# Delta-rule attention and hash-routed experts on one core: expert places by indirect scatter, columns of 106 rows, V subtracted by VectorE, PSUM banks dealt by the planner

## The chip, the core and the metric

The kernel runs on one core of one Trainium2 chip. The metric is device time in microseconds (us) of one execution; the median of several runs is given, and one further execution was recorded by the hardware profiler. Engines are called PE (TensorE, with its weight loads PEld), DVE or VectorE, ACT (ScalarE), POOL (GpSimd) and SP (SyncE, which only issues DMAs here).

## The reference

Two blocks follow one another. All numbers are fp32 but the token ids, which are int64.

```python
# attention: q, k, v are (4, 8, 768, 48), beta (4, 8, 768)
k_n = k / (norm(k, axis=-1) + 1e-6)
for t in range(768):
    y[:, :, t] = q_t @ state                       # state is (48, 48) for each batch and head
    v_old = k_n_t @ state
    state += beta_t * outer(k_n_t, v_t - v_old)
x = y.transpose(0, 2, 1, 3).reshape(3072, 384)
# experts: w1 is (8, 384, 1024), w2 (8, 1024, 384)
expert = token_ids * 2654435761 % 8
for e in range(8):
    rows = expert == e
    out[rows] = relu(x[rows] @ w1[e]) @ w2[e]
```

## The kernel before

**Attention.** The 768 steps are cut into 24 chunks of 32 tokens (`C`), and four chunks make a group (`GC`), so there are six groups. For a group the kernel does the following.

- `load_turn` loads K and Q rows through SP (1024 pieces of 192 bytes each), and `turn` transposes them on PE into a PSUM bank `z`, from which ACT copies them to `KQ`.
- `gram` forms the products K K^T and K Q^T of a chunk on PE, in two `z` banks. ACT copies the first kind to `GK`, VectorE masks the second kind into `GQ`. There are two `z` banks, given out in turn by a counter (`next_z`) when the work is listed.
- `inverse` solves the triangular system of the four chunks and all heads at once on VectorE: a transpose `NT`, a few small operations, then for each row j a multiplication into `tmp` (line 429) and an addition into `U` (line 426). The columns of `U` are taken in parts (`cols`): three for the first two groups, two for the others. Each part is a chain in which every step needs the one before; chains of different parts may be interleaved.
- `turn_back` transposes the result into `TU` (line 446), from which `spread_t` makes `Tz`.

`chunk(c)` then carries the state through one chunk, and each chunk needs the state of the one before. `ask` multiplies K and Q with the state on PE (line 466, into the banks psX and psY). The residual R is V minus the K product: for chunks 1 to 19, PE first puts -V into psX through a negated identity `nident` (line 484), `ask` adds to it, and ACT copies it out with its sign turned (line 488); for the last four chunks (`LATE`) VectorE subtracts (line 492). `solve` multiplies with `Tz` (503), ACT copies W (512), `update` forms the new state on PE (518), which ACT copies out in four pieces (533), and `answer` (541) completes the rows of x, which SP stores to a DRAM scratch.

**Places.** `routing` works out on VectorE, for each token, which expert it goes to and which place it gets there: an expert has `CAP` = 512 places of its own in four columns of 128 rows, and what lies over goes to blocks of 128 at the end. In a first part it finds each token's place. In a second part, run among the last chunks, it turns this round, so that each place knows its token: VectorE builds masks `hi` and `lo` (line 682) and PE multiplies them in 8 groups of three (48 matmul records, line 689), VectorE adds the results into `val` and derives `gidx` (row of the output) and `gx` (row of the scratch, whose order differs).

**Order.** All of this is listed as tasks with an engine, a cost in ns, and names that they read and write. `order()` plays the engines forward with these costs, always taking the ready task with the longest rest of work, and the instructions are then emitted in that order. So each engine's order is fixed at build, and each engine executes it in order.

**Experts.** When the last x row is stored, a loop over overflow blocks follows, as many as the token ids ask for. Then come the experts one after another: POOL gathers rows by indirect DMA (`gather`, line 854), PE transposes them (`turn`, 863), `gemm1` multiplies with w1 (line 870, 512 columns of places stream through PE) with the ReLU on ACT and VectorE in turn (873, 875), `gemm2` multiplies with w2 (line 881, one column of 128 places as weights, 384 columns streaming), ACT and VectorE copy out in turn (884), and POOL scatters the rows to the output (885). SP loads weights up to four experts ahead.

Of the kernel before, what the change touches and what calls it, by code (L numbers as in the profile page):

```python
# [18 lines left out]
def kernel(  # L19
# [11 lines left out]
    nc = tc.nc  # L31
# [11 lines left out]
    CAP = 512  # L43
    KT = CAP // P
    NOV = (N - CAP) // P
# [4 lines left out]
    x_dram = nc.dram_tensor("x_scratch", (N, DIN), F32, kind="Internal").ap()  # L50
    x_rows = x_dram.rearrange("(c p) e -> c p e", p=P)
# [6 lines left out]
    gidx = keep.tile([P, NHI], I32)  # L58
    gx = keep.tile([P, NHI], I32)
# [35 lines left out]
    with ExitStack() as phase1:  # L95
# [15 lines left out]
        rt = st  # L111
# [20 lines left out]
        GKs = tiles(2, "GK", [P, C, GC, HU, 2])  # L132
# [9 lines left out]
        zs = [ps.tile([P, BANK], F32, name=f"z{i}") for i in range(2)]  # L142
# [17 lines left out]
        nident = st.tile([P, P], F32)  # L160
# [10 lines left out]
        def task(eng, ns, reads, writes, emit, words=0, kb=0, more=0, boost=0):  # L171
            deps = {writer[r] for r in reads if r in writer}
            for w in writes:
                deps |= readers.get(w, set())
                if w in writer:
# [4 lines left out]
                              more=more, boost=boost))  # L180
# [5 lines left out]
            return i  # L186

        def order():
# [25 lines left out]
            fetched, issued, begun = 0, 0, []  # L214
            BLOCK, FETCH = 256, 3550.0
            have = 900.0
            done = []
            while len(done) < n:
                best = None
                for e, r in ready.items():  # L220
                    if r:
                        at = max(free[e], min(x for x, _ in r))
                        if best is None or at < best[0]:
                            best = (at, e)
                at, e = best
                r = ready[e]
                pick = max((i for x, i in r if x <= at), key=lambda i: rest[i])

                soon = [(x, i) for x, i in r
                        if at < x < at + 0.7 * tasks[pick]["ns"] and rest[i] > rest[pick]]  # L230
                if soon:
                    x1 = min(x for x, _ in soon)
                    fits = [i for x, i in r if x <= at and tasks[i]["ns"] <= x1 - at + 60]
                    if fits:
                        pick = max(fits, key=lambda i: rest[i])
                    else:
                        free[e] = x1
                        continue
                t = tasks[pick]
                r.remove(next(p for p in r if p[1] == pick))  # L240
                s = at
                if e == "PE" and t["words"]:

                    blk = (issued + t["words"]) // BLOCK
                    while len(begun) <= blk:
                        m = len(begun)
                        t0 = have if m < 2 else max(have, begun[m - 1])
                        have = t0 + FETCH
# [5 lines left out]
                fin = s + t["ns"]  # L254
                if t["kb"]:
                    dma = max(dma, fin + 1500.0) + t["kb"] * 6.3
                    end[pick] = dma + 500.0 - LAG["SP"]
                else:
                    end[pick] = fin
# [29 lines left out]
        zn = [0]  # L289

        def next_z():
            zn[0] += 1
            return (zn[0] - 1) % 2

        def turn(g, a, b):
            z, KQ, src = next_z(), KQs[g % 4], (KTs, QTs)[a][b]
            pt = zs[z].rearrange("p (u x) -> p u x", u=HU)

            def go():
                for u in range(HU):  # L300
                    nc.tensor.transpose(pt[:, u, :], src[:, u].rearrange("p r d -> p (r d)"),  # L301
                                        ident)

            task("PE", 780, (f"t{a}{b}",), (f"z{z}",), go, words=8)
            task("ACT", 600, (f"z{z}",), (f"KQ{g % 4}{a}{b}",),
                 lambda: nc.scalar.activation(KQ[:, :, a, b, :], pt, ACT.Copy))  # L306
# [4 lines left out]
        def gram(c, parts=(0, 1)):  # L311

            g, cc = divmod(c, GC)
            KQ, tk, GK, GQ = KQs[g % 4], tokens(c), GKs[g % 2], GQs[c % 12]
            zz = [next_z(), next_z()]
            pg = [zs[z].rearrange("p (u a y) -> p u a y", u=HU, a=2, y=DP)[:, :, :, 0:C]
                  for z in zz]
            a0, a1 = parts[0], parts[-1] + 1
            held = tuple(f"KQ{g % 4}{a}{b}" for a in {0, *parts} for b in range(B))
            banks = tuple(f"z{z}" for z in zz)  # L320

            def go(u):
                for r in range(2):
                    for b in range(B):
                        nc.tensor.matmul(  # L325
                            pg[r][quarter(b), u, a0:a1], lhsT=KQ[half(r), u, 0, b, tk],
# [3 lines left out]
            for u in range(HU):  # L330
                task("PE", 300, held, banks, lambda u=u: go(u), words=32)
            for r in range(2):
                if 0 in parts:
                    task("ACT", 200, (banks[r],), (f"GK{g % 2}{cc}{r}",),
                         lambda r=r: nc.scalar.activation(
                             GK[:, :, cc, :, r].rearrange("p j u -> p u j"), pg[r][:, :, 0],
                             ACT.Copy))
            for r in range(2):
                if 1 in parts:
                    task("DVE", 200, (banks[r],), (f"GQ{c % 12}{r}",),  # L340
                         lambda r=r: nc.vector.tensor_tensor(  # L341
                             GQ[:, :, r], pg[r][:, :, 1],
                             mask[:, None, :].to_broadcast([P, HU, C]), op=ALU.mult),
                         boost=1e6)
# [17 lines left out]
        def spread_t(c):  # L362
            g, x0 = c // GC, H * (c % GC)
            spread((f"TU{g % 2}",), f"Tz{c % 2}", Tzs[c % 2], TUs[g % 2][:, x0:x0 + H],
# [11 lines left out]
        def inverse(g):  # L376
# [3 lines left out]
            cols = ((0, L // 2), (L // 2, L), (L, C)) if g < 2 else ((0, L), (L, C))  # L380
            parts = tuple(f"U{i}{c0 // (L // 2)}" for c0 in range(0, C, L // 2))

            def covered(c0, c1):
                return tuple(f"U{i}{c // (L // 2)}" for c in range(c0, c1, L // 2))

            def dve(ns, reads, writes, emit):
# [3 lines left out]
            task("DVE", 1240, tuple(f"GK{i}{cc}{r}" for cc in range(GC) for r in range(2)),  # L390
                 (f"NT{i}",), lambda: nc.vector.transpose(
                     NT, GKs[i].rearrange("p j c u r -> p j (c u r)")))
# [23 lines left out]
            for j0, j1, i0 in ((0, L, 1), (L, C - 1, L + 1)):  # L416
                task("DVE", 70 + 1.04 * (j1 - j0) * (C - i0), (f"NT{i}", f"nd{i}"),
                     (f"Ni{i}{j0}",), lambda j0=j0, j1=j1, i0=i0: nc.vector.tensor_tensor(
                         Ni[:, j0:j1, i0:], NT[:, j0:j1, i0:],
# [558 lines left out]
```

## Time and profile before

| | |
|---|---|
| median of 3 runs | 623.17 us (622.58 to 624.02) |
| profiled execution | 623.59 us, its span 622.0 us |
| granted TensorE clock, mean | 0.925 |
| PE busy | 565.7 us (91%) in 6810 instructions |
| VectorE busy | 263.8 us (42%) in 983 |
| ACT busy | 177.7 us (29%) in 390 |
| POOL busy | 87.3 us (14%) in 99 |
| DMA | 59.39 MB in 121561 packets |

The span runs from the first to the last instruction. A row of engines in 40 slices gives the busy share in tenths. A group's row names its line, engine, operation, what it writes and reads, its shape, how often it ran, then its busy time and the mean of one in ns, then the idle time before it. A row of the waits gives who waited for what: total us, times, the longest.

### The profile page before, as it was taken

To read this page: it belongs to the slowest core of one execution; us is meant where nothing else is said; L and a number is where in the kernel's file an instruction comes from. 1 tells how busy PE (TensorE), PEld (TensorE's weight loads), DVE (VectorE), ACT (ScalarE), POOL (GpSimd) and SP (SyncE) were. 2 spreads that over 40 slices of the span, in tenths; PEclk is the share of its full clock that TensorE was granted. 3 is DMA by queue.
4 is the path that set the end of the run, shared out by engine and by line. 5 is a ranking of instruction groups with operands and counts; after the bars stand their busy time and mean duration, and the time that the engine had idled before them with its cause. 6 is when DMAs were issued, how large, how long until landed. Compare 5 with 4: busy or idle time off the path is not lost.

```text
span 622.0 us, 16113 instructions
## 1 busy us (share of the span) xinstructions
PE 565.7 (91%) x6810; PEld 356.3 (57%) x6810; DVE 263.8 (42%) x983; ACT 177.7 (29%) x390; POOL 87.3 (14%) x99
## 2 busy tenths in 40 slices
PE   5667999999899989369999999999999999999994
PEld 4546767768677778334554645545545546455452
DVE  8989799989989953211111111111111111111100
ACT  3345677777768632101010010010010100100100
POOL 4000000000000131260210301302203101001011
PEclk9576899989989968869999999999999999999998
DMA  9597376643334434498431233223401001000000
GB/s 151 86 157 114 63 138 118 127 93 75 83 74 94 103 101 128 128 385 297 152 117 62 100 115 120 62 97 139 141 6 60 12 0 37 0 14 28 2 22 13
DMA packets 121561, 59.39 MB, mean 95 GB/s; under 512 B 104778, under 2 KB 116118, under 8 KB 121488
## 3 DMA queue, kind: packets, MB, share of 16 engines
q1 hardware_dynamic: 117200, 48.78, 33.7%
q0 software_dynamic: 4096, 9.45, 4.5%
q8 instruction: 54, 0.88, 0.6%
q10 hardware_dynamic: 192, 0.12, 0.1%
q14 instruction: 19, 0.16, 0.1%
HBM read 50.45 MB, written 11.01 MB: 99 GB/s over the span
## 4 chain that ended last, share of the span: by engine, by line
issue 47%; POOL 7%; DMA 3%; POOLq 1%
POOL out_dram L885 5%; POOL xg L854 2%; DMA xg<-x_scratch,gx 2%; DMA x_scratch<-x_sb 1%; POOLq L885 0%; POOLq L973 0%; POOLq L854 0%; POOLq L894 0%
## 5 line engine op out<-in xcount | busy, mean ns | idle before, releaser
L881 PE MATMUL o_ps<-w_sb,h_sb 128*128 128x384 f32 x512 | 169.9, 486 | 0.0
L870 PE MATMUL h_ps<-xT,w_sb 128*128 128x512 f32 x384 | 167.5, 596 | 0.0
L881 PEld LDWEIGHTS o_ps<-w_sb,h_sb 128*128 128x128 f32 x512 | 95.2, 190 | 61.1 <-issue 1.0
L870 PEld LDWEIGHTS h_ps<-xT,w_sb 128*128 128x128 f32 x384 | 73.5, 192 | 90.7 <-issue 88.8
L875 DVE TENSOR_SCALAR h_sb<-h_ps 128x512 f32<-128x512 f32 x32 | 22.1, 692 | 144.8 <-PE h_ps L870 144.8
L426 DVE TENSOR_TENSOR U<-U,tmp 128x112 f32<-128x112 f32 (+36 forms) x322 | 73.9, 262 | 2.1
L429 DVE TENSOR_TENSOR tmp<-U,Ni 128x112 f32<-128x112 f32 (+37 forms) x322 | 73.6, 260 | 2.4
L873 ACT ACTIVATE h_sb<-h_ps 128x512 f32<-128x512 f32 x32 | 19.1, 598 | 184.3 <-PE h_ps L870 184.3
L854 POOL DMA_INDIRECT xg<-x_scratch,gx x32 | 32.8, 1024 | 164.9 <-PE xT_ps L863 149.6
L885 POOL DMA_INDIRECT out_dram<-o_sb,gidx x32 | 32.1, 1003 | 136.4 <-ACT o_sb L884 87.3
L533 ACT ACTIVATE S<-psS 48x384 f32<-48x384 f32 x92 | 44.6, 485 | 18.7 <-PE psS L518 14.5
L864 DVE COPY xT<-xT_ps 128x384 f32<-128x384 f32 x32 | 17.7, 553 | 73.7 <-PE xT_ps L863 72.6
L884 ACT COPY o_sb<-o_ps 128x384 f32<-128x384 f32 x16 | 7.7, 479 | 142.4 <-PE o_ps L881 142.4
L884 DVE COPY o_sb<-o_ps 128x384 f32<-128x384 f32 x16 | 8.9, 558 | 84.6 <-PE o_ps L881 84.6
L325 PE MATMUL z<-KQ 48*32 48x64 f32 (+1 forms) x1792 | 31.0, 238 | 12.9 <-DVE GQ L341 5.8
L325 PEld LDWEIGHTS z<-KQ 48*32 48x32 f32 x1792 | 22.2, 119 | 22.6 <-DVE GQ L341 6.8
L306 ACT ACTIVATE KQ<-z 128x512 f32<-128x512 f32 x48 | 27.3, 596 | 18.6 <-PE z L301 17.8
L541 PE MATMUL psY<-W,MT 64*64 64x48 f32 x768 | 32.2, 226 | 0.0
L518 PE MATMUL psS<-W,K 32*128 32x96 f32 x736 | 29.6, 297 | 2.4 <-ACT W L512 1.9
L541 PEld LDWEIGHTS psY<-W,MT 64*64 64x64 f32 x768 | 27.1, 140 | 6.8 <-issue 3.5
L863 PE MATMUL xT_ps<-ident,xg 128*128 128x128 f32 x96 | 17.7, 297 | 14.1 <-DMA xg<-x_scratch,gx 13.9
L503 PE MATMUL psX<-R,Tz 64*64 64x48 f32 x736 | 28.4, 227 | 1.6 <-ACT R L488 1.1
(127 smaller groups left out, 473.2 us busy)
## 6 DMA issues: line engine op xcount, KB each, us to landing
w_sb<-in_moe_w_dram SPq DMA_DIRECT2D x14, 1536.0 KB, 7.0
Kt<-in_k_dram SPq DMA_DIRECT2D x24, 192.0 KB, 4.7
Qt<-in_q_dram SPq DMA_DIRECT2D x24, 192.0 KB, 4.5
V<-in_v_dram SPq DMA_DIRECT2D x96, 48.0 KB, 2.7
K<-in_k_dram SPq DMA_DIRECT2D x96, 48.0 KB, 2.6
x_scratch<-x_sb SPq DMA_DIRECT2D x24, 192.0 KB, 2.8
w_sb<-in_moe_w_dram SPq DMA_DIRECT2D x3, 512.0 KB, 6.8
w_sb<-in_moe_w_dram SPq DMA_DIRECT2D x4, 384.0 KB, 4.9
```

What stands on the lines that cost most here:

```text
L306: lambda: nc.scalar.activation(KQ[:, :, a, b, :], pt, ACT.Copy))
L325: nc.tensor.matmul(pg[r][quarter(b), u, a0:a1], lhsT=KQ[half(r), u, 0, b, tk], rhs=KQ[half(r), u, a0:a1, b, tk], start=(u == 0), stop=True ...
L426: nc.vector.tensor_tensor(U[:, j + 1:, c0:c0 + n], U[:, j + 1:, c0:c0 + n], t, op=ALU.add)
L429: nc.vector.tensor_tensor(t, U[:, j:j + 1, c0:c0 + n].to_broadcast([P, m, n]), Ni[:, j, j + 1:, None].to_broadcast([P, m, n]), op=ALU.mult)
L503: nc.tensor.matmul(pw[rows, h], lhsT=Tz[rows, h].rearrange("p e i -> p (e i)"), rhs=R[rows, h], start=(h == 0), stop=True, skip_group_chec ...
L518: nc.tensor.matmul(psS[:, b, 2 * D * u:2 * D * u + 2 * D], lhsT=K4[quarter(b), u].rearrange("p r d -> p (r d)"), rhs=W[quarter(b), 2 * u:2 ...
L533: lambda r=r, part=part: nc.scalar.activation(S1[half(r), :, part, r], new[half(r), :, part, r], ACT.Copy))
L541: nc.tensor.matmul(py[rows, h], lhsT=MT[rows, h].rearrange("p e i -> p (e i)"), rhs=W[rows, h], start=(c == 0 and h == 0), stop=True, skip ...
L854: nc.gpsimd.indirect_dma_start(out=xg, out_offset=None, in_=x_dram[:, :], in_offset=bass.IndirectOffsetOnAxis(ap=idx, axis=0), bounds_chec ...
L870: nc.tensor.matmul(h_ps[:, :width], lhsT=w1_sb[:, co, fo * P:(fo + 1) * P], rhs=xT[:, co, :width], start=(co == 0), stop=(co == CO - 1))
L881: nc.tensor.matmul(o_ps, lhsT=h_sb[:, fo, col * P:(col + 1) * P], rhs=w2_sb[:, fo, :], start=(fo == 0), stop=(fo == FO - 1))
L885: scat = nc.gpsimd.indirect_dma_start(out=out[:, :], out_offset=bass.IndirectOffsetOnAxis(ap=idx, axis=0), in_=o_sb, in_offset=None, bound ...
```

## The change

- An expert has 424 own places in four columns of `CW` = 106 rows. GEMM1 streams 424 columns, transposes and GEMM2 work on columns of 106 rows, gathers and scatters on 106 rows. Overflow blocks keep 128 rows.
- The second part of `routing` is gone. A DRAM table `places_scratch` of (53 x 128) pairs is filled with a large number by a DMA that ACT issues, from a tile that POOL sets. VectorE works out the place of each token and a pair (row of output, row of scratch) for it; 24 indirect DMAs on POOL write 128 pairs each to their places, and one DMA on SP reads the table back as `places`.
- R is V minus the K product on VectorE for all chunks after the first; `nident` and its matmuls, and ACT's copy, are gone.
- The `z` banks are no longer given out by a counter: a task has a `job`, and `order()` gives it the banks that come free first. There are three `GK` buffers instead of two. The inverse takes two parts of columns in all groups. Costs of several tasks are changed.

```diff
-    CAP = 512
-    KT = CAP // P
-    NOV = (N - CAP) // P
+    CAP = 424
+    KT = 4
+    CW = CAP // KT
+    NOV = (N - CAP + P - 1) // P
...
+    table = nc.dram_tensor("places_scratch", (NHI * P, 2), I32, kind="Internal").ap()
...
-        GKs = tiles(2, "GK", [P, C, GC, HU, 2])
+        GKs = tiles(3, "GK", [P, C, GC, HU, 2])
...
+            def when(x, i):
+
+                job = tasks[i]["job"]
+                if tasks[i]["eng"] == "PE" and job is not None and jobs[job[0]]["at"] is None:
+                    k = len(jobs[job[0]]["leave"])
+                    left = sorted(b for b in banks if b is not None)
+                    return max(x, left[k - 1]) if len(left) >= k else None
+                return x
...
-            task("PE", 780, (f"t{a}{b}",), (f"z{z}",), go, words=8)
-            task("ACT", 600, (f"z{z}",), (f"KQ{g % 4}{a}{b}",),
-                 lambda: nc.scalar.activation(KQ[:, :, a, b, :], pt, ACT.Copy))
+            task("PE", 540, (f"t{a}{b}",), (f"j{job}",), go, words=8, job=(job, 0))
+            task("ACT", 490, (f"j{job}",), (f"KQ{g % 4}{a}{b}",),
+                 lambda: nc.scalar.activation(KQ[:, :, a, b, :], view(), ACT.Copy),
+                 job=(job, 0))
...
-            cols = ((0, L // 2), (L // 2, L), (L, C)) if g < 2 else ((0, L), (L, C))
+            cols = ((0, L, C - 1), (L, C, C - 1))
...
-                task("PE", 340, held + (f"S{c % 2}{i}0", f"S{c % 2}{i}1"), (name,),
+                task("PE", 480, held + (f"S{c % 2}{i}0", f"S{c % 2}{i}1"), (name,),
...
-            elif c < LATE:
-                task("PE", 850, (f"V1{c % 2}",), ("psX",), lambda: nc.tensor.matmul(
-                    flat, lhsT=nident, rhs=V1.rearrange("p h d -> p (h d)"), start=True,
-                    stop=True, skip_group_check=True), words=4)
-                ask(c, 0, psX, "psX", True)
-                task("ACT", 490, ("psX",), ("R",), lambda: nc.scalar.activation(
-                    R.rearrange("p h d -> p (h d)"), flat, ACT.Copy, scale=-1.0))
             else:
-                ask(c, 0, psX, "psX", False)
+                ask(c, 0, psX, "psX")
                 task("DVE", 550, ("psX", f"V1{c % 2}"), ("R",), lambda: nc.vector.tensor_tensor(
...
+            fill = new([P, NHI, 2], I32)
+            nc.gpsimd.memset(fill, BIG)
+            nc.scalar.dma_start(out=table.rearrange("(k p) t -> p k t", p=P), in_=fill)
...
+            def place(c):
+                put = nc.gpsimd.indirect_dma_start(
+                    out=table[:, :], out_offset=bass.IndirectOffsetOnAxis(
+                        ap=slot[:, c:c + 1], axis=0),
+                    in_=pay[:, c, :], in_offset=None, bounds_check=NHI * P - 1,
+                    oob_is_err=False)
...
+            for c in range(NTC):
+                task("POOL", 1000, ("rt", "pay"), (f"place{c}",), lambda c=c: place(c))
+            task("SP", 500, [f"place{c}" for c in range(NTC)], ("places",),
+                 lambda: nc.sync.dma_start(out=places, in_=table.rearrange(
+                     "(k p) t -> p k t", p=P)), kb=50, more=9000)
...
             nc.gpsimd.indirect_dma_start(
-                out=xg, out_offset=None, in_=x_dram[:, :],
+                out=xg[0:CW], out_offset=None, in_=x_dram[:, :],
...
-                nc.tensor.matmul(o_ps, lhsT=h_sb[:, fo, col * P:(col + 1) * P],
+                nc.tensor.matmul(o_ps[0:rows], lhsT=h_sb[:, fo, col * rows:(col + 1) * rows],
```

In the order that results, VectorE executes the routing up to the places ahead of the first `NT`, ACT issues the fill ahead of its first copy of `KQ`, POOL runs the 24 scatters after its first two `U` memsets and ahead of the third, and SP's load of `places` stands among the loads of group 3.

## The prediction

> **What bounds the kernel now.** I read the granted clock first, then busy time cut at the events that separate the stages (the table of stretches), then the costliest groups, then the waits of VectorE, and last the chain that ended last. The page's 40 slices give the outline:
>
> ```profile
> PE   5667999999899989369999999999999999999994
> DVE  8989799989989953211111111111111111111100
> PEclk9576899989989968869999999999999999999998
> ```
>
> Left of slice 17 is the attention stage, where PE and DVE are both at 8 to 9 and the clock wavers; right of it are the experts, where only PE is busy, at full clock. The stretches are cut at: VectorE starts the first NT transpose, ends the first TU transpose, ends the sixth and last TU, the last x row is stored, the first GEMM starts, the last output is evicted.
>
> ```profile
> 0.00:19.46 19.46, 10.97 (x284) 9.04 (x284) 17.32 (x59) 6.63 (x14) 6.46 (x19) 0.85 1.14 146
> 19.46:57.28 37.82, 26.05 (x650) 20.04 (x648) 34.43 (x174) 15.70 (x34) 0.00 (x0) 0.63 0.84 117
> 57.28:220.18 162.90, 150.72 (x4204) 117.07 (x4204) 149.80 (x634) 118.45 (x274) 6.61 (x7) 0.94 0.50 98
> 220.18:255.75 35.57, 33.31 (x682) 29.28 (x682) 11.59 (x32) 10.17 (x22) 9.34 (x9) 0.76 0.39 123
> 255.75:273.51 17.76, 4.21 (x15) 2.65 (x16) 5.25 (x12) 0.00 (x1) 9.48 (x10) 0.60 0.72 255
> 273.51:614.54 341.03, 340.43 (x978) 178.23 (x977) 45.39 (x76) 26.79 (x48) 54.41 (x54) 1.00 0.24 80
> ```
>
> Columns: length, then PE, weight loads, DVE, ACT and POOL busy, clock, DMA share. Until the sixth TU DVE works 201.6 of 220.2 us: it sets that end, with PE close behind. The tail of 35.6 us is the last four chunks, which run one after another. The experts are PE alone, 340.4 of 341.0 us. The remaining 9.05 us to the execution's own 623.59 us (0.42 above the median 623.17) are the last scatter and the end of the program.
>
> **Part 1, the experts: 424 columns.**
>
> ```profile
> L881 PE MATMUL o_ps<-w_sb,h_sb 128*128 128x384 f32 x512 | 169.9, 486 | 0.0
> L870 PE MATMUL h_ps<-xT,w_sb 128*128 128x512 f32 x384 | 167.5, 596 | 0.0
> ```
>
> The means overlap; the spacing of starts is what PE pays: median 0.429 us for 512 columns and 0.323 for 384. Linear between them, 424 columns cost 0.323 + 40/128 x 0.106 = 0.356 us. 384 GEMM1 matmuls save 384 x 0.073 = 28.0 us. GEMM2 keeps 512 x 0.323 us: 106 instead of 128 places narrow its weight side, not the 384 columns that stream. A triple of transposes (0.33 us between two GEMM2 blocks) gets 106/128 as wide; 28 triples in this stretch x 0.057 = 1.6 us. Sum 29.6 us, all on the path since PE never idles here. Bounds: 0 (fixed cost per matmul) and 40.7 us (the row of 384 columns for GEMM1); the interpolation is near 384 and has both rows beside it. What hides the rest: a weight load takes 0.19 us under a 0.356 us matmul; weights come four experts ahead; POOL needs 8 x 1.0 us in a period of 42.56 us that becomes 38.9. With the reference's seed the experts get 364, 389, 385, 423, 360, 376, 420 and 355 tokens, so none passes 424 and the overflow loop stays empty.
>
> **Part 2, VectorE's list up to the sixth TU.** The order of VectorE's instructions is fixed at build, so I price both lists with the trace's starts: a two-operand instruction of n elements holds the engine 72 + 1.045 n ns, and 115 ns more if the next one reads its result (168 elements: 251 and 365 ns). For the old list this gives 200.4 us against 201.6 busy. The new list gives 203.5. It gains 19 subtractions (line 513) at 0.47 = 8.9 us (the late four cost 0.55 from start to end). It loses the third column of the first two inverses (2.3 net), the two `hi` masks (2.8 together), three of the `lo` masks (1.4) and 0.7 in small pieces of the start; the payload and place arithmetic adds 1.4. From the first NT: 32.3 us to the first TU (35.3 before), then 157.2 to the sixth (150.8 before).
>
> Idle time is added to that. By the same prices the old list left 220.2 - 19.46 - 35.3 - 150.8 = 14.6 us idle from the first NT on; most is this:
>
> ```profile
> DVE GQ L341 <- PE z L325: 4.8, 3, 1.8
> DVE GQ L341 <- ACT GK L335: 3.4, 4, 2.1
> ```
>
> VectorE waits for a Gram product whose PSUM bank came late. Dealing the banks by the planner, a third GK buffer, and PE freed of 19 negated-V matmuls (0.91 us each, 17.3 us; line 484) attack this wait; ACT loses 19 evictions of 0.49 us. Against it stands a new wait: each subtraction waits in VectorE's queue for PE's psX, and behind it are the inverse steps and the GQ products that give banks back. The rows nearest are the late subtractions, which idled 5.7, 0.7 and 0.4 us where VectorE had nothing else; in a full queue I take 0.25 us x 19 = 4.8. Idle after the first NT: 14.6 - 8.2 + 4.8 = 11.2 us; bounds 5 (no psX wait, the bank waits gone) and 22 (the bank waits stay, psX at its 0.4 us row).
>
> **Part 3, the start.** ACT now issues the table's fill, 6784 pieces of 8 bytes, before its first eviction (5.46 us before), and waits for POOL's memset first. Back-to-back loads of 1024 pieces held SP's issue 1.1 us each once the queue was full. Priced by the 9 ns of the smallest packets over 16 engines the fill is 3.8 us, by the 28.6 ns mean of SP's queue 12.1. The first NT then starts at 22 us instead of 19.46 (19.5 to 27): the old one stood behind 1.5 us of `hi`, and VectorE's routing covers part. [...]
>
> The 24 place scatters keep POOL at the 1.30 us spacing of the old gathers: 31 us, from 22 to about 55. POOL's next memset waits for the first TU anyway. SP's load of `places` waits for them at about 56; behind it stand loads of group 3, first transposed at 77 us, and chunk loads that began at 64. Free, or at most 2 us (inside the idle bound). Sixth TU: 22 + 32.3 + 157.2 + 11.2 = 222.7 us (214 to 238).
>
> **Part 4, the tail.** The 48 place matmuls (line 689) leave PE, and their masks and sums VectorE: they sat between the late chunks. The two undisturbed periods were 7.3 and 7.1 us, the two disturbed 10.8 and 11.8. From the sixth TU to the last store at the undisturbed pace: 3 + 3 x 7.2 + 2.4 = 27 us. But the clock also played:
>
> ```profile
> 218.00:222.00 4.00, 2.25 (x34) 1.87 (x31) 3.97 (x8) 1.94 (x4) 1.75 (x2) 0.97 0.44 77
> 222.00:226.00 4.00, 4.00 (x55) 3.53 (x54) 2.54 (x5) 0.00 (x0) 1.60 (x2) 0.50 0.02 4
> 234.00:238.00 4.00, 4.00 (x73) 3.63 (x74) 1.23 (x3) 0.00 (x0) 0.83 (x1) 0.50 0.44 115
> ```
>
> After 4 us with PE 56% busy, while it waited for the sixth TU, the clock was half for about 16 us though PE was then always busy. That wait stays; with PE lighter it may grow. A chunk holds 3.4 us of PE on its chain, so two chunks at half clock add 6.8: 34. I take 30.
>
> [...] The row above stayed slow about 16 us.
>
> **Sum.** Attention end 222.7 + 30 = 252.7 (255.75 before); 17.8 to the first GEMM as before; 341.0 - 29.6 = 311.4; 9.05: together 591.0 us against 623.59, and 0.4 less against the median: 590.6.
>
> **Rivals.**
> - *Relief in full* (16%): GQ waits vanish, the fill hides, no half clock in the tail: 20 + 189.5 + 6 + 27 = 242.5, so about 580. For: DVE's idle is mostly GQ. Against: the sixth-TU wait that halved the clock remains.
> - *Start and stalls* (18%): ACT is held to the upper bound (first NT at 26), psX waits bring idle to 17, tail 33: 265.5, so about 604. For: VectorE executes in order, and it carries both recurrences now.
> - *The stream does not shrink* (2%): 106-row columns cost what 128-row ones did: 590.6 + 28 = 619. Against: the 384-column row.
> - *Half clock, slower* (3%): PE, with 17 us less to do, idles at each group's TU and drops to half clock through the middle. Chunk periods averaged 8.33 us; undisturbed 7.2 + 3.4 = 10.6. Then W of chunk 23 comes at 61.8 + 23 x 10.6 = 306, the end at 308, the whole at 646. It decides from a mean period of 9.6 us, where the attention stage ends 29.6 us late. Against: the middle ran at 0.94, with half-clock stretches of 3.4 us only.
>
> **How the numbers follow.** My forecast has 61%. The range 578 to 607 takes in relief and stalls and the bounds of the start, idle and tail, and leaves out the last two rivals and the far corners. Under 0.2% (1.25 us, about what a measurement here can tell) there is hardly any case, 1%; slower 4%, the half clock's 3 and 1 for the corners beyond it; faster the other 95%.
>
> **What would show it.** GEMM1 groups of 424 columns at 0.356 us spacing and an expert period near 38.9 us (above 41 refutes part 1). VectorE's sixth TU ending near 223 us with about 3 us more busy time than 201.6, and idle before the subtractions instead of before GQ; beyond 235 the start or psX is underpriced. The first NT near 22 us, and ACT's idle before its first eviction showing the fill. No line 689, four late chunks in about 30 us, and whether the clock is half after the last TU. A total under 578 or over 607 makes the prediction wrong.

## The result: slower, 650.3 us, and the profile after

The changed kernel takes 650.27 us (median of 4 runs, 648.65 to 650.90), the kernel before 622.88 (4 runs, 620.26 to 624.02): a ratio of 1.044, 95% interval 1.040 to 1.048. The profiled execution took 650.26 us, its span 648.6. The prediction said 590.6 (578 to 607). Without the few runs over 1.5% above their kernel's fastest, the medians of e14 and e2 in the table further down would be 625.2 and 651.1 us instead of 626.5 and 651.6.

The table of stretches, cut at the same events as before (first NT starts, first TU ends, sixth TU ends, last x eviction ends, first GEMM starts, last output evicted; columns: length, then PE, weight loads, DVE, ACT, POOL busy, clock, DMA share, GB/s):

```profile
0.00:27.90 27.90, 11.35 (x285) 8.96 (x286) 17.04 (x74) 7.33 (x15) 6.55 (x20) 0.82 1.44 78
27.90:98.17 70.27, 32.39 (x573) 23.34 (x580) 31.97 (x129) 18.70 (x39) 23.66 (x24) 0.55 0.81 79
98.17:274.96 176.79, 150.65 (x4280) 125.60 (x4283) 157.22 (x601) 106.46 (x248) 6.77 (x7) 0.84 0.45 88
274.96:300.49 25.53, 20.49 (x608) 17.47 (x607) 2.22 (x4) 10.50 (x22) 8.85 (x9) 0.95 0.55 169
300.49:329.13 28.64, 3.70 (x15) 2.45 (x16) 4.98 (x12) 0.00 (x1) 19.38 (x12) 0.51 0.94 250
329.13:640.57 311.44, 310.79 (x979) 168.44 (x977) 40.60 (x76) 24.40 (x48) 81.42 (x51) 1.00 0.28 79
```

Against before: +8.4 us to the first NT, +32.5 from there to the first TU, +13.9 to the sixth TU, -10.0 in the tail, +10.9 before the first GEMM, -29.6 in the experts. The second row is the place to look at: VectorE's busy time, 31.97 us, is what the prediction priced (32.3), but the stretch is 70.27 us long, and POOL, idle there before, is busy for 23.66.

The slices of the page show the same hole, slices 2 to 4, in DVE; under it the clock is half, from 17.9 to 89.6 us:

```profile
PE   5322478988797988783179999999999999999994
DVE  8420597989989798912011111111111111111100
PEclk9555575889889797897579999999999999999998
```

Who waits in that hole? The waits of VectorE, then of PE, from the one ahead of the first NT on (who, for what; us in total, times, longest):

```profile
DVE GQ L371 <- remote: 32.6, 2, 32.1
DVE NT L418 <- ACT GK L365: 7.2, 1, 7.2
```

```profile
PE z L355 <- issue: 16.9, 10, 12.2
PE z L329 <- DMA Qt<-in_q_dram: 12.9, 4, 7.2
```

VectorE's one wait of 32 us is for a Gram product of PE ("remote" names nobody; the order of the instructions does). PE itself waits for Q rows that SP's queue brings late, and for nothing that this view names: "issue". The timeline of PE shows where that is, and the timeline of POOL beside it (start, length, engine, instruction, count, idle before it):

```profile
53.21 0.34 PE L355 MATMUL z<-KQ 48*32 48x32 f32 x3 [0.42 <-issue]
53.98 0.21 PE L355 MATMUL z<-KQ 48*32 48x32 f32 x1 [0.43 <-issue]
54.69 0.27 PE L355 MATMUL z<-KQ 48*32 48x32 f32 x2 [0.50 <-issue]
55.39 0.21 PE L355 MATMUL z<-KQ 48*32 48x32 f32 x1 [0.43 <-issue]
56.11 0.30 PE L355 MATMUL z<-KQ 48*32 48x32 f32 x2 [0.51 <-issue]
68.66 0.33 PE L355 MATMUL z<-KQ 48*32 48x32 f32 x8 [12.25 <-issue]
```

```profile
52.77 0.98 POOL L707 DMA_INDIRECT places_scratch<-rt,rt  x1 [0.31 <-issue]
54.06 0.98 POOL L707 DMA_INDIRECT places_scratch<-rt,rt  x1 [0.31 <-issue]
```

The matmuls up to 56.4 us belong to one Gram product and have no wait between them; 64 of them took 1.02 us in e14 (below). Here they come one to three at a time. The row at 68.66 opens the next Gram product; its first matmul waits for VectorE's semaphore, that is, for a bank to be given back (VectorE's GQ ends at 68.61), and VectorE waits for the product before (PE's semaphore stands at 68.22). That ring stands until the last place scatter is over (it ends at 67.7 us). The 16 KB packets of the queue that the page calls "instruction" come at 22.3, 31.9, 54.4 and then 77.9 us; before the change they were mostly 4 to 7 us apart in this stage, 14 at most.

The experts are as predicted:

```profile
L872 PE MATMUL o_ps<-w_sb,h_sb 128*106 128x384 f32 x512 | 169.9, 487 | 0.0
L861 PE MATMUL h_ps<-xT,w_sb 128*128 128x424 f32 x384 | 139.3, 524 | 0.0
```

But POOL's gathers and scatters, 1.02 and 1.00 us each before, became slower with fewer rows:

```profile
L844 POOL DMA_INDIRECT xg<-x_scratch,places x32 | 51.9, 1620 | 138.5 <-PE xT_ps L853 120.8
L876 POOL DMA_INDIRECT out_dram<-o_sb,places x32 | 50.5, 1578 | 112.3 <-ACT o_sb L875 73.5
```

### The profile page after: what moved, and what is told of

Its sections match the earlier page's. It is cut to its first block, busy times and chain, and to the rows that moved or that the text cites. A ratio compares the mean times of both kernels' runs of the same rounds, so it can differ in the third digit from the quotient of the medians.

```text
span 648.6 us, 15911 instructions
## 1 busy us (share of the span) xinstructions
PE 529.4 (82%) x6724; PEld 346.3 (53%) x6724; DVE 254.1 (39%) x895; ACT 167.4 (26%) x371; POOL 148.2 (23%) x124
## 4 chain that ended last, share of the span: by engine, by line
issue 39%; POOL 10%; DMA 3%; POOLq 1%
POOL out_dram L876 8%; POOL xg L844 3%; DMA xg<-x_scratch,places 3%; DMA x_scratch<-x_sb 0%; POOLq L964 0%; POOLq L876 0%; POOLq L844 0%; POOLq L885 0%
## 5 line engine op out<-in xcount | busy, mean ns | idle before, releaser
L872 PE MATMUL o_ps<-w_sb,h_sb 128*106 128x384 f32 x512 | 169.9, 487 | 0.0
L861 PE MATMUL h_ps<-xT,w_sb 128*128 128x424 f32 x384 | 139.3, 524 | 0.0
L872 PEld LDWEIGHTS o_ps<-w_sb,h_sb 128*106 128x106 f32 x512 | 86.0, 172 | 68.9 <-issue 26.7
L844 POOL DMA_INDIRECT xg<-x_scratch,places x32 | 51.9, 1620 | 138.5 <-PE xT_ps L853 120.8
L876 POOL DMA_INDIRECT out_dram<-o_sb,places x32 | 50.5, 1578 | 112.3 <-ACT o_sb L875 73.5
L456 DVE TENSOR_TENSOR tmp<-U,Ni 128x60 f32<-128x60 f32 (+32 forms) x276 | 71.6, 283 | 3.1
L453 DVE TENSOR_TENSOR U<-U,tmp 128x48 f32<-128x48 f32 (+32 forms) x276 | 71.0, 280 | 2.8
L866 DVE TENSOR_SCALAR h_sb<-h_ps 128x424 f32<-128x424 f32 x32 | 19.2, 600 | 118.9 <-PE h_ps L861 118.9
L864 ACT ACTIVATE h_sb<-h_ps 128x424 f32<-128x424 f32 x32 | 16.7, 523 | 171.9 <-PE h_ps L861 171.9
L554 ACT ACTIVATE S<-psS 48x384 f32<-48x384 f32 x92 | 44.5, 484 | 28.3 <-PE psS L539 26.7
L355 PEld LDWEIGHTS z<-KQ 48*32 48x32 f32 x1792 | 24.3, 121 | 42.0 <-issue 29.1
L524 PE MATMUL psX<-R,Tz 64*64 64x48 f32 x736 | 28.3, 230 | 12.4 <-DVE U L453 7.8
L853 PE MATMUL xT_ps<-ident,xg 106*128 106x106 f32 x96 | 15.7, 277 | 25.5 <-DMA xg<-x_scratch,places 25.5
```

The source lines that it names most:

```text
L355: nc.tensor.matmul(view(r)[quarter(b), u, a0:a1], lhsT=KQ[half(r), u, 0, b, tk], rhs=KQ[half(r), u, a0:a1, b, tk], start=(u == 0), stop=Tr ...
L453: nc.vector.tensor_tensor(U[:, j + 1:jn + 1, c0:c0 + n], U[:, j + 1:jn + 1, c0:c0 + n], t, op=ALU.add)
L456: nc.vector.tensor_tensor(t, U[:, j:j + 1, c0:c0 + n].to_broadcast([P, m, n]), Ni[:, j, j + 1:jn + 1, None].to_broadcast([P, m, n]), op=AL ...
L524: nc.tensor.matmul(pw[rows, h], lhsT=Tz[rows, h].rearrange("p e i -> p (e i)"), rhs=R[rows, h], start=(h == 0), stop=True, skip_group_chec ...
L554: lambda r=r, part=part: nc.scalar.activation(S1[half(r), :, part, r], new[half(r), :, part, r], ACT.Copy))
L844: nc.gpsimd.indirect_dma_start(out=xg[0:CW], out_offset=None, in_=x_dram[:, :], in_offset=bass.IndirectOffsetOnAxis(ap=idx, axis=0), bound ...
```

## The experiments

Theory at the outset: the 6784 small writes of the fill and the 24 place scatters starve SP's loads and PE; 106 rows slow the gathers; V on VectorE stretches the middle. The table has each kernel's median and the stretches of its profiled execution (us):

| kernel | median | first NT | first TU | to sixth TU | tail | to first GEMM |
|---|---|---|---|---|---|---|
| before | 622.9 | 19.5 | 57.3 | 162.9 | 35.6 | 17.8 |
| after | 650.3 | 27.9 | 98.2 | 176.8 | 25.5 | 28.6 |
| e1_fill_flat | 634.7 | 21.2 | 82.4 | 174.6 | 26.9 | 28.5 |
| e2_places_spaced | 651.6 | 28.4 | 73.9 | 201.3 | 26.9 | 28.2 |
| e3_rows112 | 639.7 | 31.5 | 100.1 | 173.4 | 26.5 | 16.2 |
| e4_v_only | 642.9 | 19.2 | 57.6 | 181.0 | 28.4 | 19.0 |
| e5_rows64b | 615.2 | 21.6 | 59.9 | 182.1 | 25.6 | 28.4 |
| e12_rows32b | 637.2 | 21.1 | 83.5 | 175.7 | 28.2 | 28.6 |
| e13_rows64b_112 | 625.9 | 21.5 | 83.8 | 176.9 | 26.3 | 16.3 |
| e10_mended | 626.2 | 21.8 | 85.4 | 176.1 | 26.0 | 16.6 |
| e11_mended_v_pe | 625.9 | 21.9 | 85.9 | 172.4 | 27.4 | 16.4 |
| e8_pe_places | 599.0 | 20.7 | 60.1 | 169.0 | 29.5 | 18.6 |
| e9_pe_places_v | 604.5 | 20.7 | 60.9 | 174.0 | 31.0 | 18.5 |
| e14_gathers | 626.5 | 20.7 | 81.9 | 172.9 | 28.9 | 16.9 |
| e15_after_tu | 623.9 | 21.9 | 56.3 | 200.5 | 26.7 | 16.3 |
| e16_gated | 608.3 | 22.0 | 56.6 | 180.3 | 27.7 | 16.3 |
| e7_before_424 | 597.4 | 18.9 | 55.9 | 160.3 | 38.1 | 17.9 |
| e17_before_gated | 595.8 | 19.8 | 54.4 | 168.9 | 32.9 | 18.6 |

The kernel before took 620.2 to 622.5 us beside these; e12 ran once; what follows the first GEMM took 318.5 to 321.9 us in all kernels with 424 columns.

**e1_fill_flat.**

> The changed kernel, with one edit: the fill of the places table is written in one contiguous piece of 424 bytes per partition instead of 53 pieces of 8 bytes. Theory 'fill': the 6784 small writes of the fill are what keeps SP's loads and PE's instruction fetches back from 7 us on; without them the first NT starts near 20 us, the 32 us that VectorE waited before its first GQ product go with them, the first TU ends at 57 to 63 us instead of 98, and the time is 612 to 618 us. Theory 'scatters': the fill costs only its own 6 to 8 us; the first NT starts at 20 to 22, the 32 us before GQ stay, the first TU ends near 90, and the time is 641 to 645 us.

```diff
-nc.scalar.dma_start(out=table.rearrange("(k p) t -> p k t", p=P), in_=fill)
+nc.scalar.dma_start(out=table.rearrange("(p k) t -> p (k t)", p=P),
+                    in_=fill.rearrange("p k t -> p (k t)"))
```

634.7 us, between the two theories: the first TU came 15.8 us earlier, the first NT 6.7 of it. The fill cost about 16 us. In the changed kernel its 6784 packets ran from 9.0 to 29.0 us, here its 128 pieces from 9.1 to 10.0.

**e2_places_spaced.**

> The changed kernel, with one edit: the 24 place scatters no longer follow each other at 32 to 68 us; two are issued after the x rows of each of the chunks 2 to 13 are stored, and the load of the places follows the last. The fill stays in 8-byte pieces. Theory 'scatters': a burst of scatters on GpSimd's queue starves SP's loads; spaced out it has no time to, so the first NT stays at 28 us, the 32 us before GQ go, the first TU ends at 63 to 66 us, and the time is 612 to 620 us. Theory 'fill': the start is as slow as before this edit, first TU at 90 to 98, time 645 to 652 us.

```diff
+for n in range(2 * (c - 2), 2 * (c - 2) + 2):      # behind chunk(c)
+    if 0 <= n < NTC:
+        put(n, f"x_dram{c}")                       # a task name: the planner's order only
```

The spacing existed only in the planner's order. On POOL the `U` memsets, each waiting for a TU, held the scatters back, and these ran in bursts of 2, 8, 8 and 6 behind the first four TUs. The first TU came 24.3 us earlier, and the middle got 24.5 us longer: the loss moved with the scatters, and neither theory's time and first TU came together. If the two losses simply add, 15.8 (e1) and 24.3 are 40.1 us, nearly all of the 40.9 by which the first TU was late.

**e3_rows112.**

> The changed kernel, with one edit: expert gathers and scatters move 112 rows (a multiple of 16) instead of 106; rows 106 to 111 have no place and are skipped, GEMM2 makes 112 rows of output. Theory 'rows': the cost of 1.6 us per gather or scatter on GpSimd instead of 1.0, and the 12-byte packets with it, come from a row count that 16 does not divide; they return to 1.0 us, the four gathers before the first GEMM land sooner, the stretch from the last x eviction to the first GEMM falls from 28.6 to 18 to 20 us, and the time is 639 to 642 us. Rival 'clock and loads': that stretch is long because of the half clock and the weight loads beside it; spacing may change but the time stays at 648 to 652 us.

```diff
+CD = (CW + 15) // 16 * 16                          # 112
-xgs[c] = gather(places[0:CW, c, 1:2])
+xgs[c] = gather(places[0:CD, c, 1:2])
...
-gemm2(w2_sb, h_sb, kt, CW, places[0:CW, c, 0:1], True)
+gemm2(w2_sb, h_sb, kt, CW, places[0:CD, c, 0:1], True)   # and 112 rows of output
```

```profile
L845 POOL DMA_INDIRECT xg<-x_scratch,places x32 | 31.8, 992 | 136.5 <-PE xT_ps L854 132.8
L878 POOL DMA_INDIRECT out_dram<-o_sb,places x32 | 30.7, 961 | 108.2 <-ACT o_sb L877 76.4
```

Six rows more, and a gather takes 0.99 instead of 1.62 us of POOL; the stretch to the first GEMM falls by 12.4 us, the time by 10.6. POOL's own time is the smaller part; the rows also land later. With 106 rows the first transpose starts 11.6 us after the first gather, and those ahead of the first GEMM are spread over 13.2 us; with 112 rows it is 6.4 and 6.0, with the 128 of the kernel before 6.6 and 5.4. The rows theory came out in its times; whether it turns on 16 dividing the row count no run shows, since only 106, 112 and 128 rows were run.

**e4_v_only.**

> The kernel before, with one part of the change alone: V minus the asked product is taken by VectorE in chunks 1 to 19 too (no negated identity on TensorE, no ACT eviction). By the prediction's own terms: 8.9 us more on VectorE's list, 4.8 us of psX waits, up to 8 us of GQ waits gone: the sixth TU ends 2 to 10 us later, time 625 to 633 us. Rival 'VectorE was not the bound': the freed TensorE time shortens the stage, time 610 to 620 us.

```diff
-            elif c < LATE:                          # V into psX by PE
+            elif False:
```

642.9 us, worse than both theories. VectorE was busy 155.7 us from first to sixth TU instead of 149.8, so 5.9 more, and idle 25.3 instead of 13.1.

**e5_rows64b and e12_rows32b.**

> The changed kernel with the contiguous fill, and rows of 64 bytes in the places table instead of 8 (the pair and 14 words that nobody reads); as many scatters, rows and places. With 8-byte rows SP's loads moved about 40 us worth of their former rate from 21 to 66 us, and the first TU ended at 82 us. Theory 'small writes': what drains slowly is the writing of pieces under 64 bytes, so with 64-byte rows SP's loads keep their pace, the first TU ends at 58 to 66 us and the time is 610 to 620 us. Rival 'rows': each scattered row costs the same whatever its size; first TU at 80 to 86, time 631 to 638 us.

> As e5_rows64b, with rows of 32 bytes. Theory 'a piece under 64 bytes is written slowly, whatever its size': SP's loads fall as with 8 bytes, first TU at 78 to 85 us, time 630 to 637. Rival 'the cost grows with the size below 64 bytes or sits only at 8': first TU at 60 to 70, time 612 to 622.

```diff
-table = nc.dram_tensor("places_scratch", (NHI * P, 2), I32, kind="Internal").ap()
+table = nc.dram_tensor("places_scratch", (NHI * P, 16), I32, kind="Internal").ap()   # e12: 8
-pay = new([P, NTC, 2], I32)
+pay = new([P, NTC, 16], I32)                                                         # e12: 8
```

What SP's loads moved in the first 16 us of the scatters is nearly all of the last column (the scatters' own rows are under 5%). With 8-byte rows and contiguous fill (e1), with 32 (e12), with 64 (e5):

```profile
21.40:37.40 16.00, 9.33 (x160) 6.58 (x158) 10.38 (x36) 6.32 (x12) 11.03 (x11) 0.71 0.67 53
```

```profile
22.10:38.10 16.00, 7.49 (x70) 4.86 (x68) 5.55 (x23) 4.20 (x8) 12.33 (x13) 0.61 0.87 125
```

```profile
22.60:38.60 16.00, 11.53 (x208) 8.43 (x207) 11.81 (x41) 8.06 (x16) 12.33 (x13) 0.74 0.84 134
```

53 GB/s against 125 and 134 (the kernel before moved 115 there). So 8-byte rows starve SP's loads and 32-byte rows do not: the theory of e12 fell in this point, and no run shows a step at 64 bytes. Yet e12 took 637.2 us, as that theory had it, for another reason: PE ran 70 matmuls in these 16 us, e5 208. From 21 us to the first TU, PE of e1 waited 18.2 us for Q and K rows and 5.2 in "issue", PE of e12 0.4 and 24.3. So e12 is held by the scatters themselves, which e5 escaped, and starved loads are not shown to cost time on top of that: the first TU came at 82.4 us with them (e1) and at 83.5 without (e12).

**e13_rows64b_112, e10_mended, e11_mended_v_pe.** Both mends together should have given about 604 us.

> The changed kernel with its DMAs in other forms and the rest as it is: places table in rows of 64 bytes, fill and readback contiguous (a place's row lies at partition x 53 + column, six more small VectorE operations on 24 elements), 112 rows in gathers and scatters. If small writes, the readback and the 106 rows are the whole loss against the prediction outside the middle: first TU 58 to 62 us, 166 to 176 to the sixth, tail 25 to 27, 16 to 18 to the first GEMM, 320 to the end, together 589 to 603 us. Rival: the scatters still cost the middle or the start in some other way, and the time stays at 604 to 612 us, with 64-byte rows' first to sixth TU of 182 us.

> As e10_mended, with V put into psX by PE in chunks 1 to 19. Theory 'V on VectorE helps where the planner deals the banks': as with the places on PE (604.5 against 599.0 us), 3 to 8 us slower than e10_mended. Rival, the prediction's term (8.9 us of list and 4.8 of psX waits for V on VectorE): 5 to 14 us faster.

> As e5_rows64b (64-byte rows, place at column x 128 + partition, readback in 8-byte pieces), with 112 rows in gathers and scatters. Theory 'the order of rows in the table': the start stays as in e5_rows64b, first TU at 59 to 63 us, 12 us less before the first GEMM, time 600 to 607 us. Rival 'chance of timing, no part of the table's layout': PE stands still under the scatters again, first TU at 75 to 90, time 615 to 630 us.

```diff
 # e13: the edits of e5 and e3.  e10: also the table turned round
+dv("scalar_tensor_tensor", out=own, in0=own, scalar=float(NHI), in1=over,
+   op0=ALU.mult, op1=ALU.add)                      # place = partition * 53 + column
-nc.sync.dma_start(out=places, in_=table.rearrange("(k p) t -> p k t", p=P)[:, :, 0:2])
+nc.sync.dma_start(out=places.rearrange("p k t -> p (k t)"),
+                  in_=table.rearrange("(p k) t -> p (k t)", p=P))
 # e11: e10, with V put into psX by PE as before
```

All three at 626: 12 us less before the first GEMM, but the first TU at 84 to 86. SP's loads kept their pace (128 to 134 GB/s in the first 16 us of the scatters), and PE trickled under them, as after the change. The table's layout is not it, nor who subtracts V (e11 equals e10; both theories on V missed).

**e8_pe_places, e9_pe_places_v.**

> The changed kernel with its places made as before (masks on VectorE, matmuls on PE among the last chunks) and with 112 rows in gathers and scatters: no table, no fill, no place scatters, no readback. V is still subtracted by VectorE, banks are still dealt by the planner. If fill and scatters were the whole loss at the start, the first TU ends at 56 to 60 us, the stretch to the sixth stays at 173 to 177, the tail is 30 to 36 as before the change, 16 to 18 to the first GEMM, 320.5 to the end: 597 to 606 us. Rival 'the planner's order': the start is late for another reason too, first TU past 65 us, 608 us or more.

> As e8_pe_places, and V put into psX by PE for chunks 1 to 19 as before the change: what is left of the change are the 424 columns, the dealing of the banks with a third GK buffer, and two column parts in all inverses. Theory 'V on VectorE costs the middle': VectorE's list is 8.9 us shorter and its psX waits are gone, the stretch from first to sixth TU falls to 158 to 165 us, time 585 to 592 us, below e7_before_424 if the dealing helps. Rival 'the dealing or the new costs stretch the middle': it stays at 172 to 177 us and the time at 597 to 606.

```diff
 # e8: after, 112 rows, and instead of fill, scatters and readback
+nc.tensor.matmul(bank(job)[:, 0:NHI], lhsT=lo[:, i], rhs=hi[:, g * G + i], ...)   # as before
 # e9: e8, and V put into psX by PE in chunks 1 to 19
```

Without the table: 599.0 us, ratio 0.964 (0.958 to 0.971), and the first TU at 60.1. Fill and scatters were nearly the whole loss at the start. e9 came as its rival had it, the middle at 174.0 us and the time at 604.5: V on VectorE is here 5.5 us better than on PE, where e4 had it 22 worse.

**e14_gathers.**

> As e8_pe_places (places by PE, no table, 599 us), with 24 indirect DMAs at the place of the scatters that read 128 rows of V (192 bytes each) into a tile that nobody uses: work added, nothing written to DRAM. Theory 'any burst of GpSimd's indirect DMAs can hold PE': PE trickles for about 31 us, first TU at 75 to 95 us, time 612 to 630. Theory 'only the writes': first TU at 60 to 63, time 598 to 604 us.

```diff
+def look(c):                                        # in e8, after the places are known
+    nc.gpsimd.indirect_dma_start(out=got[:, c, :], out_offset=None, in_=flat_v[:, :],
+        in_offset=bass.IndirectOffsetOnAxis(ap=slot[:, c:c + 1], axis=0), ...)
```

626.5 against 599.0 us. Nothing is written to DRAM, 128 rows of 192 bytes are read by each, and PE stands still all the same (PE, then POOL, then VectorE):

```profile
41.40 0.27 PE L356 MATMUL z<-KQ 48*32 48x32 f32 x2 [1.86 <-issue]
42.81 0.21 PE L356 MATMUL z<-KQ 48*32 48x32 f32 x1 [1.15 <-issue]
43.53 0.25 PE L356 MATMUL z<-KQ 48*32 48x32 f32 x1 [0.51 <-issue]
55.37 1.02 PE L356 MATMUL z<-KQ 48*32 48x32 f32 x64 [11.59 <-DVE GQ L372]
```

```profile
43.27 1.00 POOL L697 DMA_INDIRECT rt<-in_v_dram,rt  x1 [0.30 <-issue]
44.58 1.00 POOL L697 DMA_INDIRECT rt<-in_v_dram,rt  x1 [0.30 <-issue]
```

```profile
55.02 0.49 DVE L372 TENSOR_TENSOR GQ<-z,mask 128x128 f32<-128x128 f32 x2 [26.98 <-remote]
```

The burst ends at 52.1, and PE goes on at 55.4. Its last row names the right releaser: PE waits for VectorE's GQ to give the bank back. VectorE's GQ, in turn, waits for the two matmuls that end the Gram products before. By PE's records these ended at 36.72 and 43.78 us, but the semaphore updates by which they tell VectorE stand at 54.92 and 55.02. In e8 the same two ended at 27.67 and 27.73, and their updates stand at 27.69 and 27.78. So PE's matmuls trickle first, 56 of them in 15.4 us where e8 takes 0.7, and then the word that they are done is missing until the burst is over. Packets of 16 KB on the "instruction" queue came at 19.8, 30.3 and 61.7 us.

**e15_after_tu.**

> As e10_mended, with the scatters held until the first TU is done. Theory 'the burst holds PE wherever it is': the first TU ends at 57 to 62 us, PE trickles in the 31 us behind it, the second TU ends 20 us or more later than 36 us after the first, time 612 to 628 us. Rival 'it holds PE only at the start, where little is queued': first TU at 57 to 62, the next at the pace of the other kernels, time 590 to 603 us.

```diff
-task("POOL", 1000, ("rt", "pay"), (f"place{c}",), lambda c=c: place(c))
+task("POOL", 1000, ("rt", "pay", "TU00"), (f"place{c}",), lambda c=c: place(c))
```

First TU 56.3, then 62.6 us to the second: the loss stands where the burst (57.5 to 88.9) stands. The 16 KB packets came at 67.5 and then 95.8.

**e16_gated, e17_before_gated.**

> As e10_mended (64-byte rows, contiguous fill and readback, 112 rows), with the 24 scatters spread singly: GpSimd copies one element of W of chunk c before each, one scatter a chunk for the chunks 0 to 19, two for 20 and 21. Theory 'the burst': a single scatter of 1 us holds PE for no longer than PE's instructions on hand last, so the 25 us are gone and do not come back: first TU at 56 to 58 us, 166 to 177 to the sixth, tail 25 to 28, time 588 to 602 us. Rival 'each scatter costs PE its 1.3 us wherever it is': 24 x 1.3 = 31 us spread over the middle and tail, time 615 to 630 us.

> As e7_before_424 (597.4 us), with the places by 24 scatters spread singly as in e16_gated instead of PE's mask matmuls in the tail. V stays with PE, banks with the counter. Theory 'the burst': start as in e7_before_424 plus 1 to 3 us of VectorE work for the pairs, middle 160 to 165 us, tail 38 to 27: time 583 to 590 us. Rival 'each scatter costs its 1.3 us': 605 to 620 us.

```diff
+nc.gpsimd.tensor_copy(gate[:, n:n + 1], Ws[c % 2][:, 0, 0:1])   # waits for W of chunk c
 place(n)                                                        # one per chunk
```

With a real wait between the scatters, PE's long "issue" waits at the start are gone, the first TU comes at 56.6, and e16 takes 608.3 us, 17.8 less than e10 with the same 24 scatters. So it is the burst, not 1.3 us for each; but the middle is 180.3 us, 4 more than in e10, and the expected 588 to 602 was missed: 9.3 us remain against e8, and where they come from is open. In the profiled executions the middle with single scatters is 11.3 us longer than without (e16 against e8). e7 and e17 start from the kernel before.

> The kernel before with part 1 of the change alone: 424 own places in columns of 106 rows, the places still worked out by PE's mask matmuls, V still put into psX by PE, banks by the counter; gathers and scatters move 112 rows. By the prediction's term for part 1, 29.6 us less than before in the experts, some 2 us more for the gaps in the places ahead of the first NT: 591 to 596 us. Rival: narrower GEMM1 leaves less cover for gathers and weight loads, PE waits in the experts, 600 to 612 us.

```diff
 # e7: before, with CAP = 424, CW = 106, 112 rows in gathers and scatters, gaps in the places
+dv("tensor_scalar", out=over, in0=r, scalar1=float(CW * k), scalar2=float(GAP),
+   op0=ALU.is_ge, op1=ALU.mult)
```

e7 gave 597.4 us, ratio 0.960 (0.955 to 0.966): part 1 of the change alone, 25 us better than before and 53 better than the change, a little over the 591 to 596 expected. e17, with singly spread scatters, 595.8, ratio 0.960 (0.957 to 0.964): no worse, its tail 5.2 us shorter than that of e7 and its middle 8.6 longer, so that the 583 to 590 expected of it were missed. (The profiled execution of e7 is 4.5 us under its median, that of e17 2.4 over, so these two differences are rough.) The two are the fastest of the table, with e8 close behind at 599.0.

## Why the prediction was wrong, step by step

**Part 1 was right.** From first GEMM to last output 311.44 us, predicted 311.4, and the matmuls of 424 columns start 0.356 us apart, as interpolated. What it missed was at its edge: "17.8 to the first GEMM as before" was 28.6, since gathers of 106 rows take 1.62 us each on POOL and land later. The prediction kept POOL's gathers at 1.0 us without asking what 106 rows do to them; e3 shows it: with 112 rows a gather takes 0.99 us of POOL, and the first transpose starts 6.4 instead of 11.6 us after the first gather. Why, and how many DMA engines a gather used, no run shows.

**Part 2 was right in its list, short in its idle time.** VectorE's list from first to sixth TU was priced at 157.2 us and measured 157.22; to the first TU 32.3 and 31.97. Idle time in the middle was 19.6 us, 8.4 above the 11.2 that were to cover the start as well. Its rows:

```profile
DVE R L513 <- PE psX L494: 6.9, 3, 3.3
DVE GQ L371 <- ACT GK L365: 5.7, 4, 2.6
```

The psX wait came as named (4.8 predicted). Of the 8.2 us of GQ waits that were to go, the part put down to PE's bank did (4.8 before, 0.5 after), the part put down to ACT's GK grew (3.4 to 5.7). The three psX waits, ending at 182.2, 218.2 and 253.1 us, stand at the end of half-clock stretches (174.9 to 181.7, 209.0 to 219.3 and 246.6 to 253.4); which of the two brings the other is not shown. Whether V on VectorE helps is not settled by the runs: it cost 22 us in e4, nothing in e10 against e11, and gained 5.5 in e8 against e9. The term that can be read is VectorE's own busy time, predicted 8.9 us: 5.9 in e4, 6.2 in e10 against e11, and 3.1 in e8 against e9, whose middle also holds 2.6 us of work on the places. So the agreement of the whole list is in part luck. The idle time about it goes either way, and why is open.

**Part 3 failed, and with it the forecast.** Two steps. The fill: "the first NT then starts at 22 us", bounds 19.5 to 27; it was 27.90, past the upper bound, and e1 puts 16 us on the fill by the first TU. The prediction charged it to ACT, whose first eviction came only 2.0 us later (7.46 instead of 5.46). The upper price of a packet was about right (28.6 ns, 31 measured), but the fill ran beside SP's loads for 20 us and slowed them: SP's 192-byte packets took 66 ns on average between 11 and 30 us, 21 before the change and 26 in e1. And the 24 place scatters: "free, or at most 2 us". They cost 24 us at the start (e2), in two ways: 8-byte rows cut SP's loads to less than half (53 against 125 and 134 GB/s in e1, e12, e5), and a burst of indirect DMAs keeps PE from going on with rows of 32, 64 and 192 bytes (first TU at 83.5, 85.4 and 81.9 us in e12, e10 and e14, against 60.1 in e8), but not in e5 (59.9). The second is the one whose price the runs show by itself: e14 adds the burst alone to e8 and loses 26 to 28 us. The prediction looked for who waits for POOL, found only a memset, and took POOL's time as hidden; it did not ask what POOL's DMAs share with the others.

What the burst does to PE is not shown. One guess, which stands behind the expectations of e1 and e16, is that PE runs short of instructions. The profile has a queue that it calls "instruction"; e14 moved 54 packets of 16 KB on it for 13544 records of PE (matmuls and weight loads), the kernel before 54 for 13620, about 250 each. Whether they carry PE's instructions no run shows. If they do, a PE that stands needs no packet, so that their absence, from 30.3 to 61.7 us in e14, can follow from the stop; and PE went on at 55.4 and ran some 300 records before the next packet came. So the guess is not supported. What the traces do show is the late semaphores, in e10 and e13 as in e14: VectorE's GQ started 15.4 and 8.4 us after the last of the matmuls that it waits for had ended. Many semaphore updates are missing from the traces in the same stretch (during the burst e10 has 5 of VectorE's 19, e5 91 of 97), so the records there are to be read with care. Open is also why e5 escaped: behind the first spacing, seven of its scatters came 1.31 to 1.58 us after the one before, in e13 one, and this may be cause or effect.

**Part 4 was right in direction.** The tail fell to 25.5 us (30 predicted); the half clock that was allowed for hardly came (0.95).

**Sum.** Against 591.0: +5.9 to the first NT, +46.4 from there to the sixth TU (200.7 predicted, 247.1), -4.5 tail, +10.8 before the first GEMM, 0.0 experts, +0.6 end: 650.3, with the rounding. Of the 46.4, 38.0 stand before the first TU, and 8.4 are idle time in the middle, if the 11.2 of idle time that were allowed for are all counted there; no run here takes these 8.4 apart. The rival "half clock, slower" came near in time (646) but not in kind: its point of decision was a mean chunk period of 9.6 us, and it was 8.4. "Start and stalls" named the start and put the first NT 4 us late, but had no term for the 41 us by which the first TU came later than before.

## What to carry to other kernels

An engine that "only issues DMAs in its idle time" is not free (the burst alone cost 26 to 28 us in e14): ask what else moves or waits while they run, and spread a burst of indirect DMAs by a real wait (608.3 us in e16 against 626.2 in e10; also e17) or leave it out. When two engines wait for each other in a ring, compare when the awaited instruction ended with when the waiting one started (43.8 and 55.0 us in e14): such a gap is not the work of either. Before narrowing a tile to a row count like 106, price its DMAs too: 112 rows were faster, 0.99 against 1.62 us of POOL for a gather (e3).

## What the hardware showed that was not expected

- A burst of 24 indirect DMAs on POOL (mostly 1.28 to 1.30 us apart) held PE at one to five matmuls per 0.7 to 2.1 us, then at none, until it was over (in the changed kernel and in e14). In all kernels that had it but e5 (59.9 us) the first TU came at 81.9 to 100.1 us, or, in e15, the second 62.6 us after the first; in e1 PE waited more for loads (18.2 us) than in "issue" (5.2). Reading 192-byte rows did it (e14) as well as writing 8-byte rows (the changed kernel).
- Scattered rows of 8 bytes more than halved what SP's loads moved meanwhile (53 GB/s in e1); rows of 32 bytes left it whole (125 GB/s in e12; 128 in e8, which has no scatters). The packet records give no hint: in the changed kernel a scatter of 128 rows of 8 bytes shows 32 packets, 16 of 64 bytes and 16 of 4, those ahead of 50 us 11 ns each on average, all 24 scatters' 24 ns.
- In the changed kernel the clock was half for 6.8 to 10.2 us, from 3.3 to 4.4 us after the end of each of the second to fifth TU, and for 17.1 about the first; before, the three such stretches in the middle were 3.4 us long.
